# A fixed engine order, token-major mask rows turned by DMA, and paced MoE steps in a sparse-attention + MoE kernel on one core

## Chip, cores and metric

The kernel runs on one core of one Trainium2 chip. The metric is device time in microseconds (us) of that core, as the median of the runs of a kernel; every ratio to the kernel before uses runs of the fast state on the same chip in the same rounds. Where two changed kernels are set against each other, their medians may come from different rounds, in which the kernel before took 339.4 to 339.84. The granted clock is the share of full TensorE clock that the chip allowed. Engines: PE is TensorE (matmul), PEld its weight load, DVE is VectorE, ACT is ScalarE, POOL is GpSimd, SP is SyncE, which here only issues DMAs.

## The reference

Block-sparse attention for 4 batches, 8 heads, 768 tokens, head dimension 64, with a mask in blocks of 32 tokens (neighbours, first and last row and column, and three drawn blocks per row). Its output, 3072 tokens by 512, goes through an MLP of width 2048 (the code calls it MoE).

```python
scores = scale * np.matmul(q, k.transpose(0, 1, 3, 2))
mask = np.abs(blk_i - blk_j) <= 1                       # blocks of 32
mask |= (blk_i == 0) | (blk_j == 0) | (blk_i == 23) | (blk_j == 23)
# ... plus 3 drawn key blocks per query block
attn = softmax(np.where(mask, scores, -1e9)) @ v
x = attn.transpose(0, 2, 1, 3).reshape(3072, 512)
h = x @ w_in                                            # 512 x 2048
g = h * (1.0 / (1.0 + np.exp(-beta * h)))
return g @ w_out                                        # 2048 x 512
```

## The kernel before

The mask is a product: 24 more rows in the contraction, a one-hot block index beside k and a mask row (0 or -30000) beside q, so that a score matmul contracts over 64 + 24 = 88 rows. k and q of a pair of heads are cast to fp16, turned (transposed) on PE in six 128x128 blocks, and copied by VectorE to tiles "A" and "B", one for each head. Tiles of 256 or 512 tokens go through score steps `sc` -> `et`, then `av`, then `xtp`. The MoE work of a finished tile (16 h steps: `hp` -> `t_sb` -> `g`; then o steps: `op` -> `osb`) is laid between the score steps of the next. (`sc` are scores, `et` their exponentials, `av` the product with v, `xst` the same divided by the softmax sum, `xtp` and `xt` its transpose; `hp` is h, `t_sb` its tanh, `g` the gated h, `op` and `osb` the output.) The order of instructions on each engine is the scheduler's.

```python
for i in range(NSET):                                  # 5 sets
    for nm in ("kA", "qA", "kB", "qB"):
        four[nm] = persist.tile([P, S], FP16, name=f"{nm}_{i}")
    nc.gpsimd.memset(four["kB"][0:D, :], 0.0)
    nc.gpsimd.memset(four["qB"][0:D, :], 0.0)
# ... cut
def emit_prep(b, j):                                   # one pair of heads
    # ... mask rows of the set copied in, the first 5 times
    for name, st32 in (("k", kst), ("q", qst)):
        nc.vector.tensor_copy(out=st16..., in_=st32...)              # cast
        for c in range(NC):
            nc.tensor.transpose(out=tp[:, c, :], in_=st16[:, c]..., identity=identity)
        nc.vector.tensor_copy(out=four[f"{name}A"][0:D, :], in_=flat[0:D, :])
        nc.vector.tensor_copy(out=four[f"{name}B"][D:P, :], in_=flat[D:P, :])
    nc.vector.tensor_copy(out=va[:, :, :, 0:D], in_=vst...)
# ... cut
per = len(backlog) / max(1, len(a_steps))              # MoE steps per attention step
for s in a_steps:
    if s[0] == "prep":
        prep_upto(seq.index((s[1], s[2])) + 1)
    else:
        s[1]()
    acc += per
    while acc >= 1.0 and backlog:
        backlog.pop(0)()
        acc -= 1.0
```

The softmax here doesn't subtract the row's maximum and nothing guards it: scores larger than these inputs give would overflow.

## Time and profile before

| | before |
|---|---|
| time, median of 3 (range) | 339.25 us (339.03 to 339.56) |
| span of the profiled run, granted clock | 337.4 us, 0.998 |
| PE busy / DVE / ACT / POOL | 298.4 / 181.7 / 215.8 / 28.0 us |
| first score matmul / first `hp` matmul | 21.7 / 52.7 us |
| DMA packets, of these under 512 B | 20880, 1380 |
| hardware DMA queue, share of the 16 engines | 21.8% |

The span is the time from the first to the last instruction of the profiled run. "Busy" counts a matmul's modelled latency, so 88% busy is not 88% of peak. The lines themselves are in the prediction.

### The profile page before, as it was taken

Reading aid. Unit: us, or ns where it says so; the run is one execution under the profiler, and the core shown is the slowest. Engines: PE = TensorE matmul, PEld = TensorE weight load, DVE = VectorE, ACT = ScalarE, POOL = GpSimd, SP = SyncE. Lnnn points to the kernel's source line nnn. Section 1 sums busy time; section 2 is a strip of 40 time slices with the busy share of each in tenths; the row PEclk is TensorE's granted clock in tenths of the full one; section 3 lists DMA queues with packets and bytes.
Section 4 is the critical chain, followed back from the end, with each engine's and each line's share of the span. In section 5 each row is a group of like instructions: output and inputs, shape, how many; then the busy total and the mean of one; then the engine's idle time right before and its main releaser. Section 6 shows DMA issues by size and latency. Waiting matters only on the chain.

```text
span 337.4 us, 6399 instructions
## 1 busy us (share of the span) xinstructions
PE 298.4 (88%) x2659; PEld 172.2 (51%) x2659; DVE 181.7 (54%) x408; ACT 215.8 (64%) x297; POOL 28.0 (8%) x48
## 2 busy tenths in 40 slices
PE   0055589999999999999999999999999999999995
PEld 0034466655555555555566445455455455555662
DVE  3989764543787451557866366115667114561360
ACT  1011389985998545978554989665986756954561
POOL 9994000000000000000000000000000000000000
PEclk9999999999999999999999999999999999999999
DMA  7999994112530340021340000011000010001101
GB/s 242 384 228 225 267 330 179 50 47 80 161 97 11 123 130 33 31 79 64 96 157 31 33 0 2 31 38 58 1 3 0 33 62 33 0 2 62 64 2 62
DMA packets 20880, 29.78 MB, mean 88 GB/s; under 512 B 1380, under 2 KB 17780, under 8 KB 20852
## 3 DMA queue, kind: packets, MB, share of 16 engines
q1 hardware_dynamic: 16512, 25.17, 21.8%
q0 software_dynamic: 4224, 4.19, 7.5%
q8 instruction: 21, 0.34, 0.4%
q14 instruction: 7, 0.06, 0.1%
q10 hardware_dynamic: 116, 0.01, 0.0%
HBM read 27.27 MB, written 6.29 MB: 99 GB/s over the span
## 4 chain that ended last, share of the span: by engine, by line
PE 64%; DVE 16%; ACT 14%; issue 4%; DMA 2%; SPq 0%; ACTq 0%; DVEq 0%
PE op L313 23%; PE hp L294 16%; PE sc L234 12%; PE av L260 9%; ACT et L240 8%; ACT t_sb L299 6%; DVE g L301 4%; PE tp L209 2%; PE xtp L274 2%; DMA qst<-in_q_dram 2%; DVE q_203 L204 1%; DVE va_70 L217 0%; DVE xst L266 0%; DVE qB_157 L214 0%; DVE qB_139 L214 0%
## 5 line engine op out<-in xcount | busy, mean ns | idle before, releaser
L240 ACT ACTIVATE et<-sc 128x1024 f16<-128x1024 f32 (+1 forms) x160 | 146.8, 953 | 80.4 <-PE sc L234 80.2
L313 PE MATMUL op<-w_out_sb,g 128*128 128x512 f16 x384 | 97.0, 379 | 0.1
L294 PE MATMUL hp<-xT_sb,w_in_sb 128*128 128x512 f16 (+1 forms) x448 | 95.6, 348 | 1.0 <-DVE g L301 0.2
L301 DVE SCALAR_TENSOR_TENSOR g<-t_sb,hp 128x512 f16<-128x512 f16 (+1 forms) x112 | 67.1, 610 | 44.9 <-ACT t_sb L299 44.4
L299 ACT ACTIVATE t_sb<-hp,beta_h_sb 128x512 f16<-128x512 f32 (+1 forms) x112 | 69.8, 653 | 12.1 <-PE hp L294 10.9
L294 PEld LDWEIGHTS <-w_in_sb 128*128 128x128 f16 x448 | 42.2, 97 | 35.9 <-issue 1.9
L260 PEld LDWEIGHTS <-et 128*128 128x128 f16 x1152 | 44.2, 99 | 21.6 <-DVE xst L266 10.4
L313 PEld LDWEIGHTS <-g 128*128 128x128 f16 x384 | 34.9, 97 | 33.2 <-DVE qB_163 L214 0.4
L265 DVE RECIPROCAL recip<-av 128x2 f32<-128x2 f32 (+1 forms) x64 | 11.2, 176 | 70.3 <-PE av L260 70.0
L318 ACT ACTIVATE osb<-op 128x512 f32<-128x512 f32 x24 | 14.3, 598 | 23.2 <-PE op L313 19.7
L266 DVE TENSOR_TENSOR xst<-av,recip 128x128 f16<-128x128 f32 (+1 forms) x64 | 22.8, 357 | 1.6
L276 DVE COPY xT_sb<-xtp 128x256 f16<-128x256 f16 (+1 forms) x32 | 11.5, 358 | 14.6 <-PE xtp L274 14.6
L274 PEld LDWEIGHTS <-xst 128*128 128x128 f16 x96 | 6.4, 97 | 12.5 <-DVE xst L266 12.2
L260 PE MATMUL av<-va_70,et 128*128 128x65 f16 x216 | 9.6, 199 | 2.8 <-DVE xst L266 2.7
L234 PE MATMUL sc<-qB_139,kB_138 128*128 128x256 f16 (+1 forms) x48 | 11.6, 344 | 0.5 <-ACT et L240 0.5
L274 PE MATMUL xtp<-identity,xst 128*128 128x128 f16 x96 | 10.9, 222 | 1.0 <-DVE xst L266 0.9
L234 PE MATMUL sc<-qA_137,kA_136 88*128 88x256 f16 (+1 forms) x48 | 11.1, 344 | 0.5 <-ACT et L240 0.3
L180 PE MATMUL mkx<-onehot,mask_121 24*24 24x512 f16 (+1 forms) x2 | 0.8, 506 | 10.3 <-DVE mask_121 L126 10.3
L260 PE MATMUL av<-va_72,et 128*128 128x65 f16 x216 | 9.5, 196 | 0.0
L234 PE MATMUL sc<-qB_145,kB_144 128*128 128x256 f16 (+1 forms) x36 | 8.8, 348 | 0.9 <-ACT et L240 0.9
L234 PE MATMUL sc<-qA_143,kA_142 88*128 88x256 f16 (+1 forms) x36 | 8.7, 350 | 0.6 <-ACT et L240 0.6
L234 PE MATMUL sc<-qB_163,kB_162 128*128 128x512 f16 (+1 forms) x36 | 8.5, 325 | 0.7 <-ACT et L240 0.7
(206 smaller groups left out, 249.4 us busy)
## 6 DMA issues: line engine op xcount, KB each, us to landing
kst<-in_k_dram SPq DMA_DIRECT2D x16, 384.0 KB, 4.7
qst<-in_q_dram SPq DMA_DIRECT2D x16, 384.0 KB, 5.5
vst<-in_v_dram SPq DMA_DIRECT2D x16, 384.0 KB, 5.4
out_dram<-osb SPq DMA_DIRECT2D x24, 256.0 KB, 2.0
w_in_sb<-in_moe_w_in_dram POOLq DMA_DIRECT2D x4, 512.0 KB, 10.1
w_out_sb<-in_moe_w_out_dram POOLq DMA_DIRECT2D x4, 512.0 KB, 21.7
sb_i_95<-in_sampled_blocks_dram ACTq DMA_DIRECT2D x1, 0.3 KB
beta_sb<-in_moe_beta_dram ACTq DMA_DIRECT2D x1, 8.0 KB, 4.5
```

The costliest lines, as they stand in the source:

```text
L234: nc.tensor.matmul(sc[:, i * n:(i + 1) * n], lhsT=kx[0:rows, (kc0 + i) * P:(kc0 + i + 1) * P], rhs=qx[0:rows, q0:q0 + n], start=True, stop ...
L240: nc.scalar.activation(out=et[:, 0:kn * n], in_=sc[:, 0:kn * n], func=AF.Exp, bias=0.0, scale=SCALE)
L260: nc.tensor.matmul(av[:, qc, :], lhsT=et[:, i * n + qc * P:i * n + (qc + 1) * P], rhs=va[:, hh, kc, 0:D + 1], start=(kc == 0), stop=(kc == ...
L265: nc.vector.reciprocal(out=recip[:, 0:nq], in_=av[:, 0:nq, D])
L266: nc.vector.tensor_tensor(out=xstage[:, 0:nq, hh * D:(hh + 1) * D], in0=av[:, 0:nq, 0:D], in1=recip[:, 0:nq].to_broadcast([P, nq, D]), op= ...
L274: nc.tensor.transpose(out=xtp[:, qc, :], in_=xstage[:, qc, :], identity=identity)
L276: nc.vector.tensor_copy(out=xT_sb[:, j, b * S + q0:b * S + q0 + n], in_=xtp[:, 0:nq, :].rearrange("p c s -> p (c s)"))
L294: nc.tensor.matmul(hp[:, 0:n], lhsT=w_in_sb[:, c, f * P:(f + 1) * P], rhs=xT_sb[:, c, t0:t0 + n], start=(c == 0), stop=(c == NPAIR - 1))
L299: nc.scalar.activation(out=t_sb[:, 0:n], in_=hp[:, 0:n], func=AF.Tanh, bias=0.0, scale=beta_h_sb[:, f:f + 1])
L301: nc.vector.scalar_tensor_tensor(out=g[:, f, 0:n], in0=t_sb[:, 0:n], scalar=1.0, in1=hp[:, 0:n], op0=ALU.add, op1=ALU.mult)
L313: nc.tensor.matmul(op, lhsT=g[:, f, ts * P:(ts + 1) * P], rhs=w_out_sb[:, f, :], start=(f == 0), stop=(f == N_FFC - 1))
L318: nc.scalar.activation(out=osb, in_=op, func=AF.Copy, bias=0.0, scale=0.5)
```

## The change

Its intent: start earlier, with POOL out of VectorE's way; take the turning of k and q off PE and VectorE; and let nothing but the program text decide the order on each engine. Two more things change with it: a score step of a 256-token tile holds four matmuls instead of three (144 `et` in all instead of 160), and tiles 3 and 4 no longer share their h steps (512 `hp` matmuls instead of 448). The diff, cut to its core:

```diff
+    ctx.enter_context(tc.manual_schedule())            # each engine follows the text
-    # 5 sets of kA, qA, kB, qB; POOL clears, copies mask rows, builds onehot
+    k_rows = [persist.tile([P, 2, NC, P], FP16, name=f"kr_{i}") for i in range(3)]
+    q_rows = [persist.tile([P, 2, NC, P], FP16, name=f"qr_{i}") for i in range(3)]
+    for t in k_rows + q_rows:
+        nc.vector.memset(t[:, :, :, KR:P], 0.0)
+    def mask_columns(x, which):                        # mask beside each token, once
+        for c in range(NC):
+            nc.tensor.matmul(ps[:, c, :], lhsT=oh_c[:, c, :], rhs=x, start=True, stop=True)
+        ...                                            # copied to 3 tiles by VectorE
+    def turn_by_dma(i):                                # pairs 4 to 15
+        for rows, dst in zip((k_rows[i % NST], q_rows[i % NST]), kq_tiles(i)):
+            nc.sync.dma_start_transpose(out=dst..., in_=rows...)
+    def turn_by_pe(i, which, c0, c1, on_act): ...      # pairs 0 to 3, 88 rows per head
-    # o steps in quarters (4 matmuls); osb on ScalarE
+    # o steps in halves (8 matmuls); osb on VectorE
+    cast_at = dict(zip(range(4, 16), (21, 25, 28, 32, 48, 53, 57, 63, 86, 92, 98, 104)))
+    for x in range(max(due) + 1):
+        steps[x]()                                     # one score step
+        ...                                            # av, casts, turns due at this step
+        carry += rate                                  # MoE work owed per score step
+        got = feed(carry)                              # h and o steps in alternation
```

## The prediction

> **What bounds the kernel now.** I read the page first (busy shares, 40 slices, costliest groups), then the chain of waits, then the timeline of the first 34 us and of 84 to 104 us, then matmul counts in 10 us stretches.
>
> ```profile
> PE 298.4 (88%) x2659; PEld 172.2 (51%) x2659; DVE 181.7 (54%) x408; ACT 215.8 (64%) x297; POOL 28.0 (8%) x48
> ...
> PE   0055589999999999999999999999999999999995
> ```
> TensorE is busy nearly everywhere except in the first six slices (some 50 us). "Busy" counts the modelled latency of each matmul, so I need the pitch of back-to-back ones. The chain gives it, as whole runs on one engine:
>
> ```profile
> 6.80 3.90 DVE q_203 L204
> ...
> 72.19 0.86 PE sc L234 x4
> 73.06 0.86 PE op L313 x4
> 73.92 0.76 PE av L260 x24
> ...
> 253.69 0.70 PE tp L209 x12
> ...
> 326.58 6.92 PE op L313 x32
> ```
> So a 512-column matmul costs 0.216 us, an av matmul (65 columns) about 0.0325 and a transpose 0.058. For 256 columns I take 0.109 (see the skill below). The dense sum is: op 384 x 0.216 = 82.9; hp 320 x 0.216 + 128 x 0.109 = 83.1; sc 192 x (0.216 + 0.109) = 62.4; av 1152 x 0.0325 = 37.4; transposes (192 tp, 96 xtp) 288 x 0.058 = 16.7. Together 282.5 us of a 337.4 us span: 55 us are lost. Where? The counts by stretch show about 50 tp, 19 sc (256 wide) and 24 av before 40 us, only 5.8 us of work: **34 us are lost at the start**. The last tile's h and o steps run from 317.8 to the end, 19.6 us for 64 x 0.109 + 32 x 0.216 = 13.9: **6 us are lost at the end**. The middle, 40 to 317.8, takes 277.8 us for 262.8: **15 us are lost in the middle**, unevenly:
>
> ```profile
> 30.00:40.00 10.00, 5.25 (x47) 3.99 (x46) 9.51 (x24) 2.26 (x4) 0.00 (x0) 1.00 1.17 260
> ...
> 90.00:100.00 10.00, 9.53 (x89) 5.08 (x87) 8.11 (x15) 9.17 (x14) 0.00 (x0) 1.00 0.36 112
> ...
> 120.00:130.00 10.00, 10.00 (x91) 5.26 (x90) 3.77 (x9) 6.24 (x8) 0.00 (x0) 1.00 0.38 128
> ```
> The columns are PE, PEld, DVE, ACT, POOL. At 30 to 40 us VectorE is the bound (9.51). In a stretch of h steps (90 to 100) ACT is near full (9.17); in one of o steps (120 to 130) it has room (6.24). The timeline shows why the start is late and how fast ACT alternates:
>
> ```profile
> 14.37 0.54 DVE L204 CAST q_245<-qst 128x768 f16<-128x768 f32 x1
> ...
> 21.69 1.49 PE L234 MATMUL sc<-qA_137,kA_136 88*128 88x256 f16 x6
> ...
> 87.00 1.01 ACT L240 ACTIVATE et<-sc 128x1024 f16<-128x1024 f32 x1
> ...
> 87.90 0.69 ACT L299 ACTIVATE t_sb<-hp,beta_h_sb 128x512 f16<-128x512 f32 x1
> ...
> 88.47 1.03 ACT L240 ACTIVATE et<-sc 128x1024 f16<-128x1024 f32 x1
> ```
> The first score is at 21.7 us, after a 3.9 us cast that elsewhere takes 0.54, and a mask that is ready only at 17.3. From et to et with a t_sb between takes 1.47 us, against 0.432 + 0.864 = 1.30 us of TensorE work for one score step and one h step. ACT sets that cadence in the h stretches.
>
> **What the Trainium skill says.** (1) "TensorE: Matmul & The Clock Gate", section Back-to-back issue gap: N/2.4 + 2.5 ns. That is 215.8 ns for 512 columns, and the trace has 216, so I trust its 109 ns for 256. (2) "GPSIMD Engine Reference", Specifications: SBUF interfaces shared with VectorE. The trace agrees: the 3.9 us cast overlaps POOL's memsets, and with POOL idle the same cast takes 0.54. (3) "VectorE: DVE Perf Modes", The three transpose paths: a DMA transpose of a 128x128 block takes 1309 ns, TensorE 390. On TensorE this trace shows a pitch of 58 ns when batched. It has no DMA transpose. (4) "DMA: Bandwidth & Descriptors", Latency and other measured facts: transposes move 261 GB/s in the poor case. One k or q tile of a pair (128x1536 fp16, 393 KB) would then take 1.5 us, my estimate from that page; twelve serial blocks of 1309 ns would take 15.7 us. No run yet says which.
>
> **The change part by part.**
> *Start.* POOL loses its memsets, onehot selects and mask copies; VectorE loses maskx, the four copies per set, and their contention. The first loads are issued after two small ones on the same queue (1.39 + 0.37 us of issue in the trace), so I put k of pair 0 in at about 6.2 us and q at 8.5 (before: 4.4 and 6.8). On VectorE: 14 memsets about 2.6, one-hot and identity 1.2, some ten small mask operations 2.2, mask columns of k 0.75, cast 0.54, copies of the turned k 0.6, the same for q: the first score comes at about 11 us instead of 21.7. After it ACT goes at 1.0 us per step, but each of pairs 1 to 3 needs 1.1 us of casts and 1.7 of copies on VectorE per three steps, and pair 3 waits for its load. I allow 1.5 us of stalls. The first MoE matmul comes after 16 score steps: 11 + 16 + 1.5 = **28.5 us**.
>
> *Transposes.* 144 tp of pairs 4 to 15 leave TensorE, and batch 0 gains 48 (88 columns per head instead of 128 per pair): 96 x 0.058 = 5.6 us saved. VectorE loses 48 copies of 0.555 = 26.6 us, gains 24 osb of about 0.66 (16 us, off ACT's 14.3). Every pair is cast 11 to 15 score steps ahead of its first use and turned by DMA two steps after the cast, so the transfer should be hidden.
>
> *Middle.* From the compiled order I count the steps between arrivals of MoE work, as TensorE / ACT. ACT uses about 0.95 per et, 0.6 per 512-wide t_sb, 0.42 per 256-wide one.
> - Tile 1's scores with tile 0's MoE: h half 15.8 / 18.1, o half 15.7 / 12: 34.
> - Tile 2 with tile 1's: 45.5 (h half 22.6 / 21).
> - Tile 3: 26. Tile 4: 26. Both TensorE.
> - Tile 5 with the rest of tiles 3 and 4: 39 / 33, with two bursts of 11 h steps on ACT, +2: 41.
> - Tile 6: 46.
> - Tile 7: 34, as work is held back for it.
>
> The sum is 252.5. The fixed order puts 16 h steps against 12 score steps with av between, so neither engine waits long. Before, 22.6 of TensorE stood against 1.47 us per pair.
>
> *End.* Still h (16 steps at about 0.54, the pace of the last tile before) and then o: 1.1 (turn of x) + 8.6 + 6.9 + 3.9 (osb and store) = 20.5.
>
> Sum: 28.5 + 252.5 + 20.5 = 301.5. I add 3 us for things in line behind one another (three casts in a row hold back a g or a recip; hp, op and xtp share three banks), and 1.8 for the time over the span before (339.25 against 337.4): **306 us**, a gain of 33: 17 at the start, 6 from transposes, and about 10 from the steadier middle.
>
> **Rivals.**
> - *DMA transposes become the wait.* Buffers of rows are reused every three pairs, so a cast of pair 7 (step 32) waits for the transpose of pair 4 (step 23), about 14 us later. At 1.5 us each nothing is felt; at 15.7 us each, eight transposes for batch 1 take 126 us and score steps of tile 2 wait some 40 us: 335 to 350. The low DMA share after 60 us (mean 0.2) speaks against.
> - *The fixed order loses what it gains.* Engines stand behind one blocked instruction. Before, the middle lost 15 of 263 us; if the new one loses 18 the time is about 318. For: three banks for hp, op, xtp. Against: VectorE falls by over 10 us in all.
> - *The start is bound by loads, not VectorE.* The 0 to 40 us stretches move 240 to 330 GB/s already. Twelve loads plus weights are needed by 30 us. If pair 3 or the first weights are late, the first h comes at 34: 312.
>
> **Range and chances.** 306 is the sum; the start is good to 4 us, the middle to 6, so 297 to 318. Only slow transposes bring it near the old time: faster 0.92, same 0.05, slower 0.03.
>
> **What would show it right or wrong.** First et at 10 to 13 us; first hp at 27 to 31; tp 96 instead of 192; no PE wait on a DMA after 30 us and DMA transposes landing in under 6 us; TensorE busy in 9s from slice 4 on; ACT gaps in the h stretches gone; tail of about 20 us from the last av. A VectorE cast waiting on a kT transpose, a sc matmul waiting on one, or TensorE idling on g would prove me wrong.

## The result, and the profile after

The changed kernel took **315.13 us** (314.31 to 315.8, 4 runs) against 339.4 for the kernel before in the same rounds. The ratio is 0.9285, with a 95% interval of 0.9266 to 0.9305. Ratios here are the mean time of one kernel's fast runs over that of the other's in the same rounds, so not quite the ratio of the medians quoted. Against the prediction: faster by over 2%, as expected; inside the range of 297 to 318, but 9 us above the 306.

From the page of the changed kernel: busy time, PE's 40 slices, the hardware queue (packets, MB, share), and the landing times of the DMA transposes.

```profile
PE 287.7 (92%) x2637; PEld 174.0 (56%) x2637; DVE 163.3 (52%) x418; ACT 209.4 (67%) x276; POOL 8.7 (3%) x18
...
PE   1679998899999999999998998999999999999894
...
q1 hardware_dynamic: 54260, 34.62, 42.2%
...
kT<-kr SPq DMA_TRANSPOSE x12, 3.9
qT<-qr SPq DMA_TRANSPOSE x12, 4.0
```

The slices show PE full from the fourth on, where before it was the seventh. The price is in the queue: twice the share. From the timeline of PE (start, us, operation, and in brackets the idle time ahead of it):

```profile
11.36 1.01 PE L230 MATMUL sc<-qT,kT 88*128 88x256 f16 x4 [0.25 <-ACT qT L143]
...
32.37 0.81 PE L291 MATMUL hp<-xt,w_in_sb 128*128 128x256 f16 x4
```

The first score comes 10.3 us earlier than before, the first h step 20.3 us earlier. Where the 24.9 us between the two spans came from follows from the prediction's own unit costs and the counts of matmuls in 10 us stretches:

| part | before | after | gain | predicted |
|---|---|---|---|---|
| start, 0 to 40 us: dense work done | 5.8 us | 23.6 us | 17.8 | 17 |
| dense sum of the whole | 282.5 | 276.9 | 5.6 | 6 |
| middle: lost against dense work | 15.0 | 13.1 | 1.9 | about 10 |
| end: last tile's h and o steps | 19.6 | 20.0 | -0.4 | none named |

(By 40 us the changed kernel had done 28 hp and 48 sc of 256 columns at 0.109, 20 sc of 512 at 0.216, 146 av at 0.0325 and 108 transposes at 0.058. The middle runs from 40 us to the first h step of the last tile, at 292.5 us: 252.5 us for 276.9 - 23.6 - 13.9 = 239.4 of work.) So the start and the transposes gave what was predicted; **the middle did not**. What PE waited for in the middle (us in total, times, longest), first in the kernel before, from 40 to 317.8 us, then in the changed one, from 40 to 292.5 us:

```profile
PE sc L234 <- ACT et L240: 5.1, 14, 0.7
PE av L260 <- DVE xst L266: 0.5, 2, 0.3
PE tp L209 <- DVE g L301: 0.5, 2, 0.3
```

```profile
PE hp L291 <- DVE g L298: 2.9, 5, 1.3
PE xtp L269 <- DVE xst L258: 2.6, 7, 0.8
PE sc L230 <- ACT et L233: 2.1, 4, 0.7
PE xtp L269 <- DVE g L298: 0.6, 1, 0.6
```

The waits for ACT fell from 5.1 to 2.1 us, but those for VectorE rose from 1.0 to 6.1. (Each is counted from the modelled end of the matmul ahead, so together they are less than the 15.0 and 13.1 us that the middle lost.) The longest of them, VectorE and then PE:

```profile
47.82 0.55 DVE L116 CAST kr<-kst 128x768 f16<-128x768 f32 x1
...
49.23 0.75 DVE L298 SCALAR_TENSOR_TENSOR g<-t_sb,hp 128x256 f16<-128x256 f16 x2
...
49.70 0.60 PE L291 MATMUL hp<-xt,w_in_sb 128*128 128x256 f16 x4 [1.33 <-DVE g L298]
```

Three casts in a row (kr, qr, va, 47.82 to 49.23 us) stand ahead of a `g`, and PE stands still for 1.33 us. The waits for ACT show in the stretch in which tile 0's o steps lie between tile 1's scores. First ACT, then PE, on the timeline of the changed kernel:

```profile
54.11 2.85 ACT L233 ACTIVATE et<-sc 128x1024 f16<-128x1024 f32 x3 [1.41 <-PE sc L230]
58.74 2.85 ACT L233 ACTIVATE et<-sc 128x1024 f16<-128x1024 f32 x3 [1.77 <-PE sc L230]
63.42 2.85 ACT L233 ACTIVATE et<-sc 128x1024 f16<-128x1024 f32 x3 [1.83 <-PE sc L230]
```

```profile
56.38 1.89 PE L310 MATMUL op<-w_out_sb,g 128*128 128x512 f16 x8
58.10 0.60 PE L230 MATMUL sc<-qT,kT 88*128 88x512 f16 x2
...
59.81 0.59 PE L230 MATMUL sc<-qT,kT 88*128 88x512 f16 x2 [0.45 <-ACT et L233]
```

An o step of eight matmuls holds PE for 1.72 us (56.38 to 58.10). ACT meanwhile runs out of scores and idles 1.4 to 1.8 us; then it is behind, and PE waits 0.45 us for it. Three score steps take 4.65 us this way, against 3.92 of dense work (three score steps at 0.432, an o step at 1.73, 24 av at 0.0325 and half of an xtp of four).

### The profile page after: what moved, and what is told of

Same layout as the page of the kernel before. It is cut to its first block, busy times and chain, and to the rows that moved or that the text cites. A ratio compares the mean times of both kernels' runs of the same rounds, so it can differ in the third digit from the quotient of the medians.

```text
span 312.5 us, 6381 instructions
## 1 busy us (share of the span) xinstructions
PE 287.7 (92%) x2637; PEld 174.0 (56%) x2637; DVE 163.3 (52%) x418; ACT 209.4 (67%) x276; POOL 8.7 (3%) x18
## 2 busy tenths in 40 slices
DMA packets 58511, 39.20 MB, mean 125 GB/s; under 512 B 39012, under 2 KB 55412, under 8 KB 58484
## 3 DMA queue, kind: packets, MB, share of 16 engines
q1 hardware_dynamic: 54260, 34.62, 42.2%
## 4 chain that ended last, share of the span: by engine, by line
PE 76%; DVE 12%; ACT 8%; issue 3%; ACTq 0%; DVEq 0%
PE op L310 27%; PE hp L291 21%; PE sc L230 15%; PE av L252 10%; ACT t_sb L296 5%; DVE g L298 3%; ACT et L233 3%; PE tp L138 2%; PE xtp L269 2%; DVE xst L258 2%; DVE qr L116 1%; DVE kr L116 1%; DVE kT L145 1%; DVE osb L315 1%; DVE recip L257 1%
## 5 line engine op out<-in xcount | busy, mean ns | idle before, releaser
L233 ACT ACTIVATE et<-sc 128x1024 f16<-128x1024 f32 x144 | 145.1, 1024 | 58.7 <-PE sc L230 58.6
L291 PE MATMUL hp<-xt,w_in_sb 128*128 128x256 f16 (+1 forms) x512 | 97.0, 325 | 4.2 <-DVE g L298 2.9
L298 DVE SCALAR_TENSOR_TENSOR g<-t_sb,hp 128x256 f16<-128x256 f16 (+1 forms) x128 | 70.1, 554 | 58.9 <-ACT t_sb L296 58.2
L296 ACT ACTIVATE t_sb<-hp,beta_h_sb 128x256 f16<-128x256 f32 (+1 forms) x128 | 72.7, 583 | 25.1 <-PE hp L291 23.6
L230 PE MATMUL sc<-qT,kT 88*128 88x256 f16 (+1 forms) x384 | 85.4, 327 | 3.0 <-ACT et L233 2.8
L291 PEld LDWEIGHTS <-w_in_sb 128*128 128x128 f16 x512 | 47.4, 97 | 36.1 <-issue 7.0
L310 PEld LDWEIGHTS <-g 128*128 128x128 f16 x384 | 35.8, 97 | 38.7 <-issue 0.2
L230 PEld LDWEIGHTS <-kT 88*128 88x128 f16 x384 | 36.5, 98 | 26.9 <-issue 4.9
L252 PE MATMUL av<-va,et 128*128 128x65 f16 x1152 | 46.9, 193 | 0.4 <-DVE xst L258 0.4
L315 DVE TENSOR_SCALAR osb<-op 128x512 f32<-128x512 f32 x24 | 16.6, 692 | 35.1 <-PE op L310 33.8
L257 DVE RECIPROCAL recip<-av 128x2 f32<-128x2 f32 (+1 forms) x64 | 11.1, 173 | 40.6 <-PE av L252 40.3
L271 DVE COPY xt<-xtp 128x256 f16<-128x256 f16 (+1 forms) x32 | 11.3, 353 | 3.8 <-PE xtp L269 3.7
L269 PEld LDWEIGHTS <-xst 128*128 128x128 f16 x96 | 7.0, 97 | 10.9 <-DVE xst L258 7.9
L116 DVE CAST qr<-qst 128x768 f16<-128x768 f32 x16 | 9.1, 569 | 0.0
```

What stands on the lines that cost most here:

```text
L116: nc.vector.tensor_copy(out=dst[:, :, :, 0:D], in_=st.rearrange("p h (c d) -> p h c d", d=D))
L230: nc.tensor.matmul(sc[:, i, :], lhsT=kT[0:KR, hh, kc * P:(kc + 1) * P], rhs=qT[0:KR, hh, q0:q0 + n], start=True, stop=True)
L233: nc.scalar.activation(out=et, in_=sc, func=AF.Exp, bias=0.0, scale=SCALE)
L252: nc.tensor.matmul(at[:, qc, :], lhsT=ets[(hh, kc)][:, qc * P:(qc + 1) * P], rhs=va[:, hh, kc, 0:D + 1], start=(kc == 0), stop=(kc == NC - 1))
L269: nc.tensor.transpose(out=xtp[:, qc, :], in_=xst[:, qc, :], identity=identity)
L291: nc.tensor.matmul(hp[:, 0:n], lhsT=w_in_sb[:, c, f * P:(f + 1) * P], rhs=xt[:, c, 0:n], start=(c == 0), stop=(c == NPAIR - 1))
```

## Experiments

The start of the first h step's ScalarE instruction (`t_sb`), and the time from each tile's first `t_sb` to the next tile's, counted in sixteens on the timeline, for one profiled run of each kernel.

| kernel | time | first t_sb | tile 0 to 1 | 1 to 2 | 2 to 3 | 3 to 4 | 4 to 5 | 5 to 6 | 6 to 7 |
|---|---|---|---|---|---|---|---|---|---|
| changed | 315.13 | 33.2 | 36.7 | 46.0 | 26.6 | 27.6 | 41.2 | 46.2 | 35.8 |
| c_pool | 319.06 | 37.9 | 36.7 | 46.0 | 26.6 | 27.6 | 41.2 | 46.2 | 35.8 |
| b_pe | 336.15 | 33.5 | 42.9 | 50.2 | 30.4 | 27.6 | 48.9 | 46.2 | 35.8 |
| g_twice | 329.27 | 33.4 | 38.5 | 58.7 | 26.6 | 27.6 | 41.2 | 46.2 | 35.8 |
| a_sched | 340.28 | 55.5 | 40.5 | 47.3 | 29.3 | 26.5 | 39.5 | 45.3 | 35.5 |
| s_loop | 325.19 | 44.1 | 36.7 | 46.0 | 26.6 | 27.6 | 41.2 | 46.2 | 35.8 |
| s_start | 347.18 | 62.1 | 40.3 | 48.1 | 29.3 | 26.5 | 39.5 | 45.3 | 35.6 |
| e_quarter | 307.89 | 33.2 | 35.1 | 45.2 | 26.6 | 26.9 | 39.2 | 45.4 | 35.3 |

With a fixed order a disturbance shows only in the stretch that it falls in; the others repeat to 0.1 us.

### c_pool: is it POOL's work that slows VectorE at the start?

```diff
 make_identity(nc, identity)
+busy = [persist.tile([P, S], FP16, name=f"busy_{i}") for i in range(2)]
+for i in range(12):
+    nc.gpsimd.memset(busy[i % 2][0:D, :], 0.0)
```

> The changed kernel with twelve extra memsets of 64x768 fp16 on POOL at the start (about 8.5 us of POOL, as the kernel before had). Theory (the start of the kernel before was long chiefly because POOL's memsets slow VectorE's casts): the casts and copies between 1 and 10 us grow from about 0.55 to 1 us and more, one of them to 2 to 4 us, the first score moves from 11.4 to 14 to 17 us, and the time grows by 3 to 6 us. Rival (the start was long for the number of VectorE steps and their order): first score within 1.5 us of 11.4 and the time within 1.5 us of the changed kernel's 315.

Measured: 319.06 us (318.91 to 319.19), ratio to before 0.94 (0.9386 to 0.9414): 3.9 us slower than the changed kernel. VectorE's timeline:

```profile
3.09 1.05 DVE L178 CAST onehot<-ident 24x768 f16<-24x768 f32 x1
...
9.09 1.17 DVE L116 CAST kr<-kst 128x768 f16<-128x768 f32 x1
...
13.11 0.55 DVE L116 CAST qr<-qst 128x768 f16<-128x768 f32 x1
```

The same form of cast takes 1.17 us while POOL clears and 0.55 once it is done. The first score comes at 14.6 us instead of 11.4, and the table puts the loss ahead of the first h step alone. Contention is real and worth about 4 us, as expected.

### k_before_dve: is that all that made the old start slow?

```diff
-        nc.gpsimd.memset(four["kB"][0:D, :], 0.0)
-        nc.gpsimd.memset(four["qB"][0:D, :], 0.0)
+        nc.vector.memset(four["kB"][0:D, :], 0.0)
+        nc.vector.memset(four["qB"][0:D, :], 0.0)
```

(In the kernel before.)

> The kernel before with its ten 64x768 memsets moved from POOL to VectorE (10 x about 0.45 us there). Theory (contention is a large part of the late start): the q cast of pair 0 falls from 3.9 us to under 1, the first score comes 2 to 5 us earlier than 21.7 and the time falls by 1 to 4 us. Rival (the number of VectorE steps sets the start): the first score is no earlier, as the memsets now stand in VectorE's own line, and the time is within 1 us of 339.

Measured: 340.04 us (338.62 to 341.71), ratio 1.0011 (0.9985 to 1.0037). The q cast that had taken 3.90 us fell to 0.54, yet the first score came later, at 25.8 us instead of 21.7. VectorE's timeline of this run says why:

```profile
20.88 0.56 DVE L217 CAST va<-vst 128x768 f16<-128x768 f32 x1 [6.79 <-DMA vst<-in_v_dram]
21.36 0.16 DVE L126 TENSOR_SCALAR mask<-mask_blk 24x24 f16<-24x24 f32 x1
```

The scheduler put a cast of v ahead of the mask's last step; the cast waits 6.79 us for its load and the mask stands behind it. "TensorE: Matmul & The Clock Gate" in the Trainium skill, section "Architectural detail: the array is 16× 32×32, not 1× 128×128", says that VectorE's and ScalarE's queues are strictly first in, first out; this trace agrees. The first score hung on the **order** on VectorE, not only on its speed. The expectation was half wrong. As the order moved along with the memsets, this run does not tell what the clears alone cost in the old text.

### a_sched and b_fixed: the fixed order taken away, and the fixed order alone

```diff
-    ctx.enter_context(tc.manual_schedule())     # a_sched: in the changed kernel
+    ctx.enter_context(tc.manual_schedule())     # b_fixed: in the kernel before
```

> The changed kernel without the line that fixes the order, so that the scheduler may move instructions. The compiled order differs little: av, xtp and tp runs are cut or moved by a step in some places. Theory (what counts is the order in which the program emits the steps, not that it is fixed): within 1 % of 315 us. Rival (the fixed order is what avoids stalls): 3 % or more slower.

> The kernel before with nothing but the fixed order added: each engine follows the text of the program. It tells whether the fixed order is a gain of its own or only carries the new text. Theory: the text of the kernel before was written for a scheduler (all set-up ahead, POOL still clears its buffers, the slow cast is still there), so the order alone gains little: 330 to 350, first score at 20 to 26 us. Rival: the fixed order is itself the gain; then under 325.

| | scheduler's order | fixed order |
|---|---|---|
| text of before | 339.6 | 444.63 (443.97 to 447.32) |
| text of the change | 340.28 (338.92 to 340.76) | 315.13 |

Without the fixed order the whole gain is gone: a_sched stands at 1.0019 (0.9997 to 1.0041) of before. That refutes the expectation, which had given the order less than 1%. And the fixed order alone is no gain but a loss of 31%: 1.3113 (1.3071 to 1.3156). Neither half explains the result; only both together do.

Why b_fixed is slow shows on PE's timeline; each prepared pair stands in line:

```profile
24.99 0.82 PE L210 MATMUL tp<-identity,k 128*128 128x128 f16 x6 [3.82 <-DVE k L205]
27.91 0.82 PE L210 MATMUL tp<-identity,q 128*128 128x128 f16 x6 [2.10 <-DVE q L205]
33.00 0.82 PE L210 MATMUL tp<-identity,k 128*128 128x128 f16 x6 [4.27 <-DVE k L205]
...
49.16 0.84 PE L261 MATMUL av<-va,et 128*128 128x65 f16 x12 [0.59 <-DVE xst L267]
```

PE waits for casts ahead of `tp` for 55.7 us in all (29.5 for q, 26.2 for k), 21.4 ahead of `xtp` and 16.1 ahead of `av`. That text has each cast, turn and use side by side and relies on a scheduler to pull them apart.

Why a_sched is slow shows on VectorE's timeline:

```profile
53.19 0.56 DVE L115 CAST kr<-kst 128x768 f16<-128x768 f32 x1 [4.46 <-DMA kst<-in_k_dram]
53.67 0.28 DVE L257 TENSOR_TENSOR xst<-av,recip 128x128 f16<-128x128 f32 x1
...
94.41 0.56 DVE L115 CAST kr<-kst 128x768 f16<-128x768 f32 x1 [4.72 <-DMA kT<-kr]
94.89 0.42 DVE L270 COPY xt<-xtp 128x512 f16<-128x512 f16 x1
```

The scheduler moves casts ahead of ready work (`xst`, `xt`). There they wait for a load, or for a DMA transpose that still reads the rows, and everything on VectorE waits with them. PE then starves, and its granted clock falls too. One stretch of both kernels, with the columns stretch, length, busy us (instructions) of PE, PEld, DVE, ACT and POOL, then granted clock, DMA share and GB/s; first without the fixed order, then with it:

```profile
50.00:60.00 10.00, 5.99 (x50) 4.66 (x51) 4.16 (x11) 3.51 (x7) 0.00 (x0) 0.66 1.16 287
```

```profile
50.00:60.00 10.00, 8.87 (x86) 4.86 (x85) 5.04 (x13) 6.49 (x8) 0.00 (x0) 1.00 1.23 259
```

How much of the loss is the clock (0.75 and 0.66 in 40 to 60 us, 0.66 in 90 to 100) and how much the waits that go before it, no run separates.

### s_start and s_loop: which part needs the order?

```diff
-    ctx.enter_context(tc.manual_schedule())
+    fixed = tc.manual_schedule(); fixed.__enter__()      # s_start
     ... set-up ...
+    fixed.__exit__(None, None, None)                     # s_start: loop left to the scheduler
+    ctx.enter_context(tc.manual_schedule())              # s_loop: only this, set-up left to it
     for x in range(max(due) + 1):
```

> The changed kernel with the fixed order for the set-up only (all that comes before the first score step of the main loop); the scheduler may order the main loop. In the trace of the version without any fixed order the first MoE matmul came 22 us late (54.2 against 32.4 us), and after it 284 us passed against 280. Theory one: the loss lies in the set-up, where casts that wait for loads were put ahead of the mask on VectorE. Then the set-up in fixed order gives most of it back: first score near 11.4 us, first MoE matmul at 33 to 37, time 316 to 324. Rival: the casts of pairs 1 to 3 and of later pairs, which belong to the loop, are hoisted in the same way and still hold VectorE; then first MoE matmul after 45 us and time over 330.

> The mirror image: the scheduler may order the set-up, the main loop is in fixed order. Theory one (the loss lies in the set-up): first score near 23 us as without any fixed order, first MoE matmul near 44 to 50, time 327 to 337. Rival (the loss lies in the loop): time 316 to 322. If both halves alone lie near 318, or both near 338, the loss is not a sum of two parts, and each half alone is not its cause.

Measured: s_start 347.18 us (346.83 to 350.03), ratio 1.0246; s_loop 325.19 (323.8 to 325.28), ratio 0.9567. For s_start the rival held, and the theory that the loss lay in the set-up's own order fell. For s_loop the 325.19 lie between the two: just under the theory's 327 to 337 and above the rival's 316 to 322. s_loop loses 10.1 us by the medians and 10.9 in the profiled run, all of it ahead of the first h step (table). Its VectorE line, the scheduler ordering the set-up only:

```profile
13.71 0.56 DVE L115 CAST kr<-kst 128x768 f16<-128x768 f32 x1 [1.88 <-DMA kst<-in_k_dram]
14.19 0.16 DVE L172 TENSOR_SCALAR ident<-dif 24x24 f32<-24x24 f32 x1
```

By the built order, three casts (k and q of pair 0, k of pair 1), each waiting for its load, stand ahead of the first step of the mask; the one shown is the third. In s_start, where the set-up is fixed and the loop free, the mask still starts behind a cast:

```profile
9.23 0.56 DVE L117 CAST kr<-kst 128x768 f16<-128x768 f32 x1 [6.53 <-DMA kst<-in_k_dram]
9.70 0.16 DVE L174 TENSOR_SCALAR ident<-dif 24x24 f32<-24x24 f32 x1
...
42.67 0.56 DVE L117 CAST va<-vst 128x768 f16<-128x768 f32 x1 [4.17 <-DMA vst<-in_v_dram]
...
56.02 0.56 DVE L117 CAST kr<-kst 128x768 f16<-128x768 f32 x1 [5.37 <-DMA kst<-in_k_dram]
```

By the built order of this kernel, the cast at 9.23 us is that of pair 1, which belongs to the loop and moved up into the set-up. The first h step comes 28.9 us late, worse than with no fixed part at all (22.3). The parts do not add, since a free loop disturbs the set-up. Past the third tile the scheduler is even a little better (a_sched: 1.0, 1.8, 0.9 and 0.2 us less in the last four columns, before rounding). So the fixed order is worth most where casts wait for loads, ahead of the first h step (22.3 us), and less in the first three columns after it (7.8 us).

### b_pe: are the DMA transposes worth it?

```diff
-                turn_by_dma(i)
+                kq_tiles(i)
+                to_turn += [(i, 0), (i, 1)]
...
+        if to_turn and not is_open[0]:              # no half-done op tile holds a bank
+            turn_by_pe(*to_turn.pop(0), 0, NC, -1)
```

> The changed kernel with pairs 4 to 15 turned on TensorE too, one tensor of a pair after a score step, instead of by DMA. It adds 288 transposes (the token-major rows need twice as many as the 144 of the kernel before) and 48 copies on VectorE. Theory (TensorE sets the time in the middle, so each transpose counts in full and the DMA's are hidden): 288 x 0.058 = 16.7 us more, range 13 to 20, so about 332 us; half of it, 8.3 us, is what the kernel before paid. Rival (the gain lies in start and order, transposes fit in gaps): under 6 us more.

Measured: 336.15 us (336.06 to 337.45), ratio 0.9913 (0.9894 to 0.9932), 21 us slower than the changed kernel: as predicted in kind, and above the range of 13 to 20. PE has 288 more instructions and 18.5 us more busy time, VectorE 22.2 us more. The ScalarE wait for scores, in total us, times and longest, in the waits of this run and then of the changed kernel:

```profile
ACT et L233 <- PE sc L230: 77.9, 64, 3.1
```

```profile
ACT et L233 <- PE sc L230: 58.6, 51, 3.1
```

The dense price of 288 transposes is 16.7 us. The 21 us fall in just those columns of the table in which the pairs are turned. In this text, with PE in the place of the DMA, only 3 us of the gain are left. But this variant turns twice the 144 blocks that the kernel before turned for these pairs, and it tries one place for the turns; a better one might cost less. So the 21 us are the price of this alternative, not a share of the gain.

### g_twice: how much room do the DMA transposes leave?

```diff
                 turn_by_dma(i)
+                turn_again(i)          # the same two, into one scrap tile
```

> The changed kernel with each DMA transpose of pairs 4 to 15 issued twice, the second time into a scrap tile that nobody reads: 24 more transfers of 393 KB. Theory: the transposes are hidden, so the time stays within 2 us of the changed kernel (313 to 317.5). Rival: the transposes already load the queue so that loads or casts feel them; 24 more of about 4 us then cost over 5 us in all, with VectorE casts waiting on a transpose or on a load.

Measured: 329.27 us (327.56 to 330.07), ratio 0.9693 (0.9661 to 0.9725), 14.1 us slower. The time went the rival's way. The table puts 12.7 of it between tiles 1 and 2. SP issues the loads of pairs 8 and 9 behind the transposes; the first such load on SP's timeline in this run, then in the changed kernel:

```profile
93.48 0.44 SPq L108 DMA_DIRECT2D kst<-in_k_dram  x1
```

```profile
68.74 0.43 SPq L108 DMA_DIRECT2D kst<-in_k_dram  x1
```

The load is issued 24.7 us later, and VectorE, in fixed order, waits for it with everything behind it:

```profile
98.39 0.56 DVE L116 CAST kr<-kst 128x768 f16<-128x768 f32 x1 [9.87 <-DMA kst<-in_k_dram]
```

One flaw of the experiment: the repeats share one scrap tile, so SP waits 27.6 us in all for one repeat to land before the next, which plain extra traffic would not do. 10.2 us of this fall before the late load, more than the 9.87 us that the cast then waits; so the run does not show what plain extra transposes would have cost, nor whether the rival's reason is the right one. What it does show: transposes and loads share SP's line, and what holds the line delays the loads. And from the changed kernel's own list of waits: no cast and no PE instruction waits for a DMA transpose, so at their number they are hidden. How much room is left stays open.

### f_even: is the alternation worth anything?

```diff
     def choose(want_h):
-        src = (hq if want_h else oq) or hq or oq
-        ...
+        return oq if oq and (not hq or oq[0][2] < hq[0][2]) else hq
...
-            rate = todo / (n_steps - x + TAIL)
-            if nxt:
-                rate = min(rate, have / max(1, nxt[0] - x))
+            rate = have / max(1, nxt[0] - x) if nxt else todo / (n_steps - x + TAIL)
```

> The changed kernel with MoE work taken in plain order (all h of a tile, then its o) and spread evenly up to the next arrival, so neither alternation nor holding back for later tiles. Theory (both matter only for tiles 2 to 5, where TensorE is the bound under either rule): 0 to 3 us slower. Rival (alternation and pacing are the source of the steadier middle): 5 us or more slower, with ACT near full and TensorE gaps in the h stretches of tiles 3 and 4.

Measured: 315.51 us (314.65 to 316.2), ratio 0.9299 (0.9276 to 0.9323). Even spreading without alternation or hold-back is as good as the pacing of the change, as the theory (0 to 3 us slower) had it.

### e_quarter: are the large o steps what the middle loses?

```diff
-        def o_step(ts, half):       # f in range(half * 8, half * 8 + 8)
+        def o_step(ts, quarter):    # f in range(quarter * 4, quarter * 4 + 4)
...
-    [(1.72, o_step(ts, x), group) for ts in range(n // P) for x in range(2)]
+    [(0.86, o_step(ts, x), group) for ts in range(n // P) for x in range(4)]
```

> The changed kernel with o steps in four parts of 4 matmuls instead of two of 8. Theory (in tile 1's second half an o part of 1.73 us for every three score steps leaves ACT without scores, and then TensorE waits for ACT: 4.65 us per three score steps against 3.95 of dense work): 2 to 4 us faster, and the ACT gaps of 1.4 to 1.8 us between 50 and 68 us are gone. Rival (the step size is of no matter, ACT is only late at the start): within 1 us.

Measured: 307.89 us (307.62 to 309.3), ratio 0.9073 (0.9054 to 0.9092): 7.2 us faster than the changed kernel, above the 2 to 4 that were expected. ACT's timeline in the stretch shown above:

```profile
53.20 1.02 ACT L233 ACTIVATE et<-sc 128x1024 f16<-128x1024 f32 x1 [0.17 <-PE sc L230]
54.50 1.02 ACT L233 ACTIVATE et<-sc 128x1024 f16<-128x1024 f32 x1 [0.28 <-PE sc L230]
55.80 1.02 ACT L233 ACTIVATE et<-sc 128x1024 f16<-128x1024 f32 x1 [0.28 <-PE sc L230]
```

The gaps of 1.4 to 1.8 us are now 0.2 to 0.3, and PE's wait for `et` over the whole run fell from 2.8 to 0.7 us. Of the 7.2 us the table's columns hold 6.4. The change had doubled the o step, in a kernel whose two score buffers let PE be only two score steps ahead of ACT.

But this wait is not the whole of the gain. PE's waits in the middle of this run, from 40 us to the last tile's first h step at 285.5 us, to be read against the four lines of the changed kernel above:

```profile
PE hp L291 <- DVE g L298: 1.8, 3, 1.3
PE xtp L269 <- DVE xst L258: 0.6, 2, 0.3
PE xtp L269 <- DVE g L298: 0.6, 1, 0.6
```

The wait for `et` lost 2.1 us, that of `xtp` for `xst` 2.0 and that of `hp` for `g` 1.1. So the edit is shown to bring 7.2 us, of which the starved ACT is one part. The rest lies between PE and VectorE. Shorter o steps also change what lies ahead of each `xtp` and `hp`, and how often h and o alternate; no run separates that from the length of the step.

### q_tail and j_all: the remaining losses at the end and the start

q_tail is e_quarter with the last eight o quarters of tile 6 held back and laid between the last tile's h steps. j_all is q_tail with the start reordered:

```diff
     mask_columns(id16, k_rows)
+    mask_columns(mask16, q_rows)
     cast(0, "k")
     load(1, "v")
-    turn_by_pe(0, 0, 0, NC, 0)
-    mask_columns(mask16, q_rows)
     cast(0, "q")
+    turn_by_pe(0, 0, 0, NC, 0)
...
-        if x in (0, 3, 6):
-            i = x // 3 + 1
+        if x in (0, 2, 5):
+            i = (x + 1) // 3 + 1
```

> As the quarter steps, and the last eight o quarters of tile 6 are held back and put between the last tile's h steps, three more between its av steps. Theory (the last 16 h steps go at 0.54 us for latency, not for TensorE's 0.436): another 2 to 3 us off compared with the quarter steps alone. Rival (ACT and VectorE set the pace of the last h steps): no gain, or a loss as the o work comes later.

> As the last one, and the start put in another order: both sets of mask columns first, both casts of pair 0 before its turns, and pairs 2 and 3 cast one score step earlier. Theory (VectorE's order at the start costs time: it idles from 7.0 to 8.6 us, and pair 3 waits 2.1 us): first score at 9.5 to 10.5 us instead of 11.4, first h 2 to 3 us earlier, and 2 to 3 us off the time of the last one, about 308 us. Rival (loads and weights set the start): first score within 0.5 us and time within 1 us of the last one.

q_tail: 307.85 us (306.97 to 308.62), ratio 0.9063 (0.9043 to 0.9083). There is no clear gain over e_quarter, and the expected 2 to 3 us did not come. From the first `t_sb` to the end the two profiled runs take 272.6 us (e_quarter) and 271.9 (q_tail), so the new end is worth 0.7 us there; the start of the q_tail run, whose text is the same, came 1.7 us later (first `t_sb` at 34.9 instead of 33.2), which is how far one kernel's runs can differ. j_all: **305.18 us** (304.85 to 305.24), ratio 0.8983 (0.8971 to 0.8996), the fastest of all. PE's timeline of j_all:

```profile
10.02 1.01 PE L230 MATMUL sc<-qT,kT 88*128 88x256 f16 x4
...
30.51 0.81 PE L291 MATMUL hp<-xt,w_in_sb 128*128 128x256 f16 x4
```

Its first score and first h step come 1.3 and 1.9 us earlier than in the changed kernel, and the time is 2.7 us under that of q_tail, as the theory (2 to 3 us) had it.

## Why the prediction was right, and where its steps failed

The direction and range held. Of its three reasons the transposes came out in size and in mechanism, the start in size and partly by luck, and the middle not. Its sum, term by term, with stretches by the first h step on PE (tiles 3 to 5 together, as their h steps overlap):

| term | predicted | measured | difference |
|---|---|---|---|
| first MoE matmul | 28.5 | 32.4 | +3.9 |
| scores of tile 1 | 34 | 36.1 | +2.1 |
| tile 2 | 45.5 | 46.3 | +0.8 |
| tiles 3 to 5 | 93 | 95.5 | +2.5 |
| tile 6 | 46 | 46.1 | +0.1 |
| tile 7 | 34 | 36.1 | +2.1 |
| end | 20.5 | 20.0 | -0.5 |
| "in line behind one another" | 3 | in the terms above | -3 |
| time over span, profiled run | 1.8 | 1.8 | 0.0 |
| median over the profiled run's 314.31 | none | 0.8 | +0.8 |

- **The split 17, 6, 10 is not worked out in the prediction.** With the changed kernel's 16.1 us of dense work ahead of its first h step (96 transposes, 96 av, 48 sc of 256 and 8 of 512 columns, 8 xtp), the prediction's own 28.5, 252.5 + 3 and 20.5 mean gains of 22, 6, 6 and -1 for start, transposes, middle and end. The measured 17.8 for the start agrees with the named 17 by luck: the first h step came 3.9 us late. By its own terms the start fell short by about 4 us and the middle by about 4.5.
- **Start: one term too small.** The first score was right (11.4 for "about 11"). "I allow 1.5 us of stalls" was not: ACT waited 1.21, 0.55 and 2.13 us for casts and copies of pairs 1 to 3, 3.9 in all; and the four steps with the rest of q's turns took 1.25 us instead of 1.0. j_all recovers some of this by moving casts up a step.
- **The reason given for the start was incomplete.** The prediction laid the late start to POOL's contention and to VectorE's work. Contention is about 4 us (c_pool). But taking POOL's clears out of the kernel before moved nothing (k_before_dve), and the new text without the fixed order has its first score at 23.2 us, later than before. The order on VectorE, mask ahead of any cast that waits for a load, is what separates 11.4 from that 23.2. The prediction listed the fixed order as a risk; it was a condition of the whole gain (a_sched).
- **Transposes: right.** They land in 4 us (neither the 1.5 nor the 15.7 of its two estimates), no engine waits for one, and 96 transposes on PE at 0.058 are 5.6 us. The rival "DMA transposes become the wait" did not occur. How much room SP's line has left, g_twice does not settle.
- **Middle: the step that failed.** "About 10 from the steadier middle" came to 1.9. "The fixed order puts 16 h steps against 12 score steps with av between, so neither engine waits long" counted PE and ACT alone. For ACT it was in part right: PE's waits for it fell from 5.1 to 2.1 us. What it left out is VectorE, for which PE waited 6.1 us instead of 1.0: for `g`, among others behind three casts in a row, and for `xst`. The 3 us that it had allowed for such lines did not cover it. And it overlooked the o half: the steps of eight matmuls leave ACT without scores and then PE without `et`, so that where it set "o half 15.7 / 12" as PE-bound, PE also waited. e_quarter takes 7.2 us away with one edit and lowers all three waits.
- **Its own signs.** First `et` at 12.4 us, 96 tp, transposes landing under 6 us and no PE wait on a DMA came true. The first hp at 32.4 lies outside its 27 to 31, ACT's waits for scores fell over the whole run from 80.2 us to 58.6 but did not vanish, and "TensorE idling on g", one of three things that it said would prove it wrong, did happen.
- **End: right** at 20 us.
- **Pacing** had no price or worth of its own (f_even), which the prediction did not separate.

## What to carry to other kernels

A fixed engine order is neither a gain nor a loss by itself: it pays where the text already puts each cast, load and turn where its data is there, and it cost 31% here where the text had left that to a scheduler. So change the text and the order together, and test each alone before crediting either. And look at the longest piece of work laid between steps of a two-engine pipeline: where it is longer than the other engine's stock of ready work, try cutting it; here that was the largest gain that a single edit to the changed kernel brought (7.2 us). Then list what the busiest engine waits for before and after: here the change took away waits for one engine and put others, for a third engine, in their place.

## What the Trainium skill lacked or had wrong

- "VectorE: DVE Perf Modes", The three transpose paths: its 1309 ns is for one 128x128 block by DMA. Here one DMA transpose of twelve such blocks (393 KB) landed in 3.9 to 4.0 us by the median, 0.33 us per block. On TensorE, for which it gives 390 ns, the pitch of batched transposes was 58 ns in the trace before; per record they took 267 ns (k, changed kernel). A reader who multiplies the page's figures gets 15.7 us for the transfer.
- "DMA: Bandwidth & Descriptors" does not tell what DMA transposes do to other transfers of the same issuer. Here the packets rose from 20880 to 58511 (39012 of them under 512 B), the queue's share from 21.8% to 42.2%, SP needed 1.37 to 3.72 us to issue one transpose of k, and doubling them through one scrap tile, on which SP waited 27.6 us, put a load 24.7 us late (14.1 us of time). The 261 GB/s that its section Latency and other measured facts gives for transposes would make 1.5 us of the 393 KB; here they took 3.9 to 4.0 from issue to landing, about 100 GB/s with the latency in it.
- "TensorE: Matmul & The Clock Gate", Back-to-back issue gap: the formula that the prediction took stands there for an isolated matmul, and the section puts a sustained stream of 512 columns at about 131 ns each. Here 32 `op` matmuls in a row took 6.92 us, 216 ns each: the formula held, the figure for the stream did not.
- No page tells what the order on an in-order engine is worth when a cast waits for a load: in the changed text it was 25 us of 340 (a_sched).
